# A new order for five engines ahead of the second feed-forward block, a second buffer for output gates, and one state copy on VectorE

## The chip, the cores and the metric

The kernel runs on one core of a Trainium2 chip, in one launch. The time is device time in microseconds, and the median of several runs is compared. A profile shows one further execution with its instructions: PE is TensorE, DVE VectorE, ACT ScalarE, POOL GpSimd, SP the engine whose queue issues the DMAs. PEld is TensorE's weight load.

## What is computed

The reference is an mLSTM attention with a running state, then two feed-forward layers over 3072 tokens (4 batches of 768) with 320 features:

```python
for t in range(S):
    m_new = np.maximum(f_gate[:, :, t] + m, i_gate[:, :, t])
    f_stab = np.exp(f_gate[:, :, t] + m - m_new)
    i_stab = np.exp(i_gate[:, :, t] - m_new)
    m = m_new
    C = f_stab[:, :, None, None] * C + i_stab[:, :, None, None] * np.einsum('bhd,bhe->bhde', vt, kt)
    n = f_stab[:, :, None] * n + i_stab[:, :, None] * kt
    h_tilde = np.einsum('bhde,bhe->bhd', C, qt)
    nq = np.einsum('bhd,bhd->bh', n, qt)[:, :, None]
    denom = np.maximum(np.abs(nq), 1.0)
    o = 1.0 / (1.0 + np.exp(-o_gate[:, :, t]))
    y[:, :, t] = o * h_tilde / denom
...
h = np.maximum(x @ w_in, 0.0)
x = (h * h @ w_out).astype(np.float32)
...
h = x @ w_in
g = h * (1.0 / (1.0 + np.exp(-h)))
return (g @ w_out).astype(np.float32)
```

Both feed-forward layers go from 320 features to 2048 and back.

## The kernel before

**Tiles.** The attention goes by chunks of 128 tokens: 24 tiles, numbered by the list `TILES`. Tiles 0 to 17 take the batches 0, 1 and 2 in turn, chunk by chunk; tiles 18 to 23 are batch 3. Tile 18 is therefore the only tile behind the first three that begins a batch. The first feed-forward layer runs over 8 blocks of 384 tokens (three tiles), each in 16 slices `in0` to `in15` of 128 columns, and an `out` step after each; the second layer runs over 3 blocks of 1024 tokens.

**The early part.** Everything up to the end of the first block's feed-forward (400 steps) is named, and each name has a date in the table `ORDER`. The steps are sorted by date, no earlier than what they need, and written out in that order for all five engines, so each engine runs its instructions in that order and waits where its next instruction has to wait. The program behind it keeps TensorE's order by hand too.

**The names.** A step's number after a colon is its tile, one without is a slice or a weight piece.
- Gates: `ga`, `gg` are VectorE's scans (line 219, 224) over the gates, `0` for the first 128 columns, `1` for the other 640; `ta`, `tb` are TensorE's transposes of them and `tc`, `td` VectorE's copies of these (line 246).
- Attention of a tile: `q`, `v`, `w`, `e` and `sg` are loads on SP; `b0`, `b1` masks and `s` scores on TensorE (lines 435 to 518); `x0`, `x1` exponentials on ACT (line 493); `d` VectorE's products of the two (line 526); `h` TensorE's weighted sums (lines 590 to 605); `ev` their division and gating (lines 616 to 624); `si` ACT's sigmoid of the output gates (line 415); `st`, `gr`, `gm` the state, where `gr` copies it out of PSUM (line 642 on); `xt`, `xa`, `xl` the transposition into the feed-forward's `x` and its split into a high and a low part. `stk` is a stacked operand of later tiles, which SP fetches by DMAs (`sj`).
- Weights of the first layer: 16 pieces; `L` loads piece k on SP, `P` (ACT), `D` (VectorE), `C` (ACT) and `M` (VectorE or POOL) split it into two parts (from line 287). Piece 0 feeds `in0` and `in1`, piece 1 `in2` and `in3`, piece 3 `in4` and `in5`, piece 5 `in6` and `in7`, piece 11 `in12` and `in13`.
- Slice j: `in` (TensorE, line 734) into PSUM, `r` relu, `gh` high part, `g` square (each on ACT, or `g` on VectorE or POOL), `gl` low part on VectorE (line 758), then `out` (lines 778 to 780).

**Padding.** `#x n` in the table puts n matmuls on a tile of zeros ahead of step x (`pad`, line 250), written into a PSUM buffer that the step overwrites; `warm` does the same as a step of its own (line 256).

Of the kernel before, what the change touches and what calls it, by code (L numbers as in the profile page):

```python
# [12 lines left out]
ACTF = mybir.ActivationFunctionType  # L13
# [41 lines left out]
    #h:3 3 #xt:4 3 tc0 3.01 b0:0 3.02 we0 3.18 tb0 3.3 td0 3.3 x0:0 3.53 x1:0 3.63 s:0 3.73 b0:1 3.9 b1:0 3.91
    b1:1 4 #warm1 4 s:1 4.2 L2 4.73 gD0 4.8 #in2 5 b0:2 5.1 s:2 5.18 b1:2 5.2 ga1 5.4 ee0 5.98 #xt:2 6 #ta1 6
    #in0 6 #in3 6 x0:1 6.1 d0:0 6.13 x1:1 6.2 #in4 7 warm1 8.02 x1:2 8.58 tb1 10.18 gb1 10.24 vk:0 10.78
    gg1 11.34 ee1 11.5 eD0 11.53 #warm7 12 gc1 12.02 gD1 12.19 eD1 12.19 ar1 13.07 x0:2 13.43 q:3 16.85 e:3 16.91
    we1 16.95 st:0 17.83 warm2 18.11 d0:1 19.97 w:3 20.45 P0 20.72 as1 20.84 wt1 20.84 ta1 20.84 d1:1 21.43
    d1:0 21.63 h0:0 21.85 h1:0 21.85 D0 22.18 vk:1 22.56 tc1 22.58 warm3 22.81 v:3 22.81 L3 23.49 h0:1 23.99  # L60
    vk:2 24.22 C0 26.17 h1:1 30.45 d0:2 31.5 td1 31.73 warm4 32.12 take 32.12 ev:0 32.4 xt:0 32.73 d1:2 32.73
    M0 32.87 sg:3 33.05 ev:1 33.8 q:4 33.92 h0:2 34.17 xa:0 34.3 P1 34.34 m1:3 34.54 m0:3 34.85 xl:0 34.92
    ev:2 35.22 h1:2 35.31 xt:1 35.48 D1 35.71 xt:2 35.72 P2 35.78 M3 36.13 mp 36.55 gr:0 37.3 xa:2 37.68
    xa:1 38.05 w:4 38.23 xl:1 38.41 warm5 38.43 L5 38.51 in0 38.51 gm:0 38.76 L4 38.83 st:1 38.88 x1:3 38.93
    e:4 39.13 xl:2 39.14 C1 39.19 M1 39.19 C2 39.28 warm6 39.31 x0:3 39.5 r0 39.55 gh0 39.55 in1 39.59 D2 39.66
    M2 39.73 g0 39.73 gl0 39.73 C3 39.75 s0:3 39.87 d0:3 39.87 gh1 39.87 P3 39.88 vv:3 39.88 r1 39.91 g1 40.14
    in3 40.17 in2 40.27 si:3 40.29 L6 40.89 out0 41.04 D3 41.13 g3 41.51 gl3 41.51 gr:1 41.97 r3 42.38 gh3 42.38
    vk:3 43.21 gl1 44.17 s1:3 44.78 m1:4 44.97 v:4 45.57 r2 46.1 P4 46.81 in4 49.09 st:2 49.18 L7 49.83 gh2 49.97
    gm:1 50.07 qt:3 50.24 P5 50.37 m0:4 50.44 D4 50.55 g2 50.82 d1:3 50.84 r4 50.89 gh4 50.89 q:5 50.94
    gr:2 51.16 vv:4 51.34 D5 51.43 C4 51.57 M4 51.73 g4 52 gm:2 52.19 gl4 52.23 gl2 52.57 in5 52.61 x0:4 52.91  # L70
    P6 53.16 C5 53.21 h:3 53.22 out1 53.27 D6 53.39 out2 53.73 ev:3 53.74 C6 54.24 M5 54.27 st:3 54.6 L8 54.81
    r5 54.83 m0:5 54.94 M6 55.46 w:5 55.46 P7 55.72 x1:4 56.86 gr:3 56.92 gm:3 56.92 in6 56.93 r6 57.24 gh6 57.24
    g6 57.24 L9 57.75 L10 59.56 P8 59.75 D7 59.78 m1:5 59.82 gl6 60.05 D8 60.25 xt:3 60.31 s0:4 60.36 C7 60.38
    d0:4 60.47 e:6 60.53 gh5 60.56 g5 61.18 gl5 61.18 x0:5 61.41 s1:4 61.58 d1:4 61.58 C8 61.68 M8 61.68
# [5 lines left out]
    gl9 70.23 r10 70.32 P12 70.33 P11 70.95 g10 71.2 v:6 71.38 gm:4 71.81 out8 71.98 q:7 72.53 gh10 72.55  # L80
    out7 72.61 xa:4 72.71 sj:6 72.74 d1:5 72.98 D11 73.07 C11 73.07 D12 73.19 C12 73.21 M12 73.21 M11 73.41
    st:4 73.61 gr:4 73.61 P13 73.7 in12 73.8 r12 73.83 D13 74.47 r11 74.86 gl10 75.12 g12 75.29 h:5 75.48
    gh12 75.52 P14 76.12 D14 76.12 C13 76.53 vk:5 76.55 g11 76.56 g13 76.78 in13 77.01 r13 77.02 M13 77.08
    gl11 77.18 gh11 77.29 gh13 77.39 m0:6 77.46 out9 77.54 gl13 77.55 out10 77.7 w:7 77.77 C14 77.79 in14 77.91
# [1317 lines left out]
```

## Time and profile before

| | us |
|---|---|
| runs | 803.69, 805.22, 806.42; median 805.22 |
| profiled execution | 803.72 |
| its span (first to last instruction) | 802.0 |
| TensorE busy | 794.4 |
| VectorE busy | 588.1 |
| ACT busy | 506.1 |
| POOL busy | 65.6 |
| granted clock of TensorE, mean | 1.00 |

The profile comes from the one execution of 803.72 us, so a sum made from its rows is made against that time. Times in rows count from the start of the span. An instruction's row on TensorE includes the part in which the next one already runs; how long a step holds the engine is therefore read from start to start.

### The profile page before, as it was taken

To read this page: it belongs to the slowest core of one execution; us is meant where nothing else is said; L and a number is where in the kernel's file an instruction comes from. 1 tells how busy PE (TensorE), PEld (TensorE's weight loads), DVE (VectorE), ACT (ScalarE), POOL (GpSimd) and SP (SyncE) were. 2 spreads that over 40 slices of the span, in tenths; PEclk is the share of its full clock that TensorE was granted. 3 is DMA by queue.
4 is the path that set the end of the run, shared out by engine and by line. 5 is a ranking of instruction groups with operands and counts; after the bars stand their busy time and mean duration, and the time that the engine had idled before them with its cause. 6 is when DMAs were issued, how large, how long until landed. Compare 5 with 4: busy or idle time off the path is not lost.

```text
span 802.0 us, 15413 instructions
## 1 busy us (share of the span) xinstructions
PE 794.4 (99%) x5671; PEld 748.0 (93%) x5671; DVE 588.1 (73%) x1117; ACT 506.1 (63%) x1018; POOL 65.6 (8%) x92
## 2 busy tenths in 40 slices
...
GB/s 259 241 249 277 174 160 194 223 212 254 237 229 257 230 226 252 193 240 236 200 107 128 239 204 219 200 181 162 45 152 129 154 152 121 80 142 128 64 34 34
DMA packets 110961, 144.63 MB, mean 180 GB/s; under 512 B 39567, under 2 KB 81431, under 8 KB 110887
## 3 DMA queue, kind: packets, MB, share of 16 engines
...
q8 instruction: 45, 0.74, 0.4%
...
## 4 chain that ended last, share of the span: by engine, by line
PE 94%; ACT 2%; DMA 2%; SPq 1%; issue 0%; DVE 0%; ACTq 0%
PE hin L734 21%; PE mC L875 15%; PE o L991 7%; PE o L990 7%; PE o L992 7%; PE o L778 7%; PE o L779 7%; PE o L780 7%; PE mA L875 3%; PE hA L605 2%; PE sc L518 2%; PE hA L590 2%; PE mO L875 1%; PE hA L600 1%; PE st L640 1%; PE xT L674 1%
## 5 line engine op out<-in xcount | busy, mean ns | idle before, releaser
L734 PE MATMUL hin<-x,wi 128*128 128x384 f32 x1024 | 203.2, 340 | 0.0
L734 PEld LDWEIGHTS hin<-x,wi 128*128 128x128 f32 x1024 | 177.6, 188 | 0.8 <-ACT r L742 0.2
L778 PE MATMUL o<-wo,gh 128*128 128x320 f32 x384 | 120.8, 315 | 0.0
L779 PE MATMUL o<-wo,gh 128*128 128x320 f32 x384 | 118.7, 309 | 0.0
L990 PE MATMUL o<-wo,gh 128*128 128x320 f32 x384 | 118.6, 309 | 0.0
L991 PE MATMUL o<-wo,gh 128*128 128x320 f32 x384 | 118.6, 309 | 0.0
L992 PE MATMUL o<-wo,gl 128*128 128x320 f32 x384 | 118.5, 309 | 0.0
L780 PE MATMUL o<-wo,gl 128*128 128x320 f32 x384 | 118.5, 308 | 0.0
L875 PE MATMUL mC<-xa,wp 128*128 128x512 f32 x396 | 113.6, 395 | 0.0
L742 ACT ACTIVATE r<-hin 128x384 f32<-128x384 f32 x128 | 61.9, 485 | 66.5 <-PE hin L734 66.2
L875 PEld LDWEIGHTS mC<-xa,wp 128*128 128x128 f32 x396 | 73.8, 189 | 15.7
L758 DVE TENSOR_TENSOR gl<-r,gh 128x384 fp32r<-128x384 f32 x128 | 70.5, 560 | 19.7 <-ACT r L753 19.3
L991 PEld LDWEIGHTS o<-wo,gh 128*128 128x128 f32 x384 | 72.2, 188 | 1.3
L990 PEld LDWEIGHTS o<-wo,gh 128*128 128x128 f32 x384 | 72.1, 188 | 1.3
L778 PEld LDWEIGHTS o<-wo,gh 128*128 128x128 f32 x384 | 72.1, 188 | 0.4 <-issue 0.2
L779 PEld LDWEIGHTS o<-wo,gh 128*128 128x128 f32 x384 | 72.2, 188 | 0.1
L780 PEld LDWEIGHTS o<-wo,gl 128*128 128x128 f32 x384 | 72.1, 188 | 0.0
L992 PEld LDWEIGHTS o<-wo,gl 128*128 128x128 f32 x384 | 72.1, 188 | 0.0
L746 ACT ACTIVATE gh<-r 128x384 fp32r<-128x384 f32 x128 | 67.2, 525 | 3.8
L753 ACT ACTIVATE r<-r 128x384 f32<-128x384 f32 x125 | 65.6, 525 | 3.9
L889 ACT ACTIVATE r<-c 128x512 f32<-128x512 f32 x24 | 15.2, 632 | 66.6 <-DVE c L911 66.6
L911 DVE TENSOR_TENSOR c<-u,mC 128x512 f32<-128x512 f32 x44 | 30.0, 687 | 33.7 <-PE mC L875 33.7
...
## 6 DMA issues: line engine op xcount, KB each, us to landing
...
```

The costliest lines, as they stand in the source:

```text
L734: pe.matmul(ps[:, 0:N], w[:, c, ws], x[:, sl, 0:N], start=(k == 0), stop=(k == 7))
L742: act.activation(out=r, in_=ps, func=ACTF.Relu)
L746: act.activation(out=gh, in_=r, func=ACTF.Square)
L753: act.activation(out=r, in_=r, func=ACTF.Square)
L758: on("gl", t0 // L).tensor_tensor(out=gl, in0=r, in1=f(gh), op=ALU.subtract)
L778: pe.matmul(o[k][:, 0:DM], gh[:, c], w[:, 0:320], start=first, stop=False)
L779: pe.matmul(o[k][:, 0:DM], gh[:, c], w[:, 320:640], start=False, stop=False)
L780: pe.matmul(o[k][:, 0:DM], gl[:, c], w[:, 0:320], start=False, stop=last)
L875: pe.matmul(o, w, x, start=start and k == 0, stop=k == 3, skip_group_check=True)
L990: pe.matmul(o[k][:, 0:DM], gh[:, t], w[:, 0:320], start=first and x == 0, stop=False)
L991: pe.matmul(o[k][:, 0:DM], gh[:, t], w[:, 320:640], start=False, stop=False)
L992: pe.matmul(o[k][:, 0:DM], gl[:, t], w[:, 0:320], start=False, stop=last and x == len(js) - 1)
```

## The change

It has four parts.

**1. The table `ORDER` is new**, all 400 dates. Two rows of it, for the look of it:

```diff
-    b1:1 4 #warm1 4 s:1 4.2 L2 4.73 gD0 4.8 #in2 5 b0:2 5.1 s:2 5.18 b1:2 5.2 ga1 5.4 ee0 5.98 #xt:2 6 #ta1 6
+    0.7 c0 0.92 warm7 0.94 #b0:0 1 #h:1 1 q:1 1.57 #warm9 2 c4 2.37 v:1 2.88 #xt:2 3.0 #in4 3.0 sg:0 3.35 c2 3.43
```

The padding matmuls go from 75 to 16:

| | before | after |
|---|---|---|
| ahead of the first gate transpose | `warm7` 12, `warm8` 1 | `warm7` 6, `warm9` 2 |
| up to `in0` | `b0:1` 2, `s:1` 1, `s:2` 3, `warm1` 4, `warm2` 2, `h:1` 3, `xt:2` 6, `st:1` 2, `in0` 6 | `b0:0` 1, `h:1` 1, `xt:2` 3 |
| behind it | `in1` 1, `in2` 5, `in3` 6, `in4` 7, `st:2` 3, `h:3` 3, `xt:3` 1, `s:4` 2, `s:5` 1, `xt:4` 3, `st:4` 1 | `in4` 3 |

What it does to the start of the program on SP, whose queue issues every load, is seen in its first rows. `kq` are keys and queries of a tile, `vk` and `x` values, `sg` output gates, `raw` a weight piece of 768 KB and `ro` one of 640 KB; the first `raw` before is piece 0, then 1. Before:

```order
L411 DMA sg<-in_og_dram 128x3x320
L387 DMA kq<-in_qkn_dram 40x2x512 x4
L402 DMA vk<-in_vk_dram 128x656 x2
L387 DMA kq<-in_qkn_dram 40x2x512 x2
L402 DMA x<-in_vk_dram 128x656
L268 DMA raw<-in_w_in_dram 128x1536 x2
L281 DMA ro_260<-in_w_out_dram 128x1280
L232 DMA g_d<-gg 32x128
L233 DMA e_d<-eg 32x128
```

After (the first `raw` is piece 1, the second piece 0):

```order
L386 DMA kq<-in_qkn_dram 40x2x512 x2
L401 DMA vk<-in_vk_dram 128x656
L410 DMA sg<-in_og_dram 128x3x320
L386 DMA kq<-in_qkn_dram 40x2x512 x4
L267 DMA raw<-in_w_in_dram 128x1536
L401 DMA vk<-in_vk_dram 128x656
L231 DMA g_d<-gg 32x128
L280 DMA ro_209<-in_w_out_dram 128x1280
L401 DMA x<-in_vk_dram 128x656
L267 DMA raw<-in_w_in_dram 128x1536
L231 DMA g_d<-gg 32x640
```

The load of piece 0 moved behind those of piece 1 and of the first `ro`.

On VectorE the long scans moved. Rows of the gates before (`COPY aw` is `tc0` and `td0`, `32x640` the other 640 columns):

```order
L228 TENSOR_TENSOR a_r<-a_r,gg 32x128
L229 TENSOR_TENSOR w_a<-a_r,gg 32x128
L246 COPY aw<-gT 128x32 x2
L219 SCALAR_TENSOR_TENSOR w_r<-fg,w_r,a_r 32x640
L526 TENSOR_TENSOR W<-sc,W 128x512
L221 TENSOR_TENSOR fg<-fg,w_r 32x640
L560 TENSOR_TENSOR vk<-vk,aw 128x320
L222 TENSOR_TENSOR fg<-fg,w_r 32x640
L224 SCALAR_TENSOR_TENSOR gg<-eg,fg 32x640
```

After:

```order
L218 SCALAR_TENSOR_TENSOR w_r<-fg,w_r,a_r 32x640
L227 TENSOR_TENSOR a_r<-a_r,gg 32x128
L220 TENSOR_TENSOR fg<-fg,w_r 32x640
L221 TENSOR_TENSOR fg<-fg,w_r 32x640
L226 TENSOR_TENSOR a_r<-a_r,w_r 32x640
L228 TENSOR_TENSOR w_a<-a_r,gg 32x128
L223 SCALAR_TENSOR_TENSOR gg<-eg,fg 32x640
L245 COPY aw<-gT 128x32
L227 TENSOR_TENSOR a_r<-a_r,gg 32x640
L525 TENSOR_TENSOR W<-sc,W 128x512
```

Both scans over 640 columns now stand ahead of the first `COPY aw`.

TensorE's row just ahead of the first feed-forward matmul (`hin`), before, from the transposition of tile 2 on; `wz` is the tile of zeros, and of the six pads ahead of `hin` the first is shown:

```order
L674 MATMUL xT<-ident,y 128x128 x2
L677 MATMUL xT<-ident,y 64x128 x2
L250 LDWEIGHTS wz
L250 MATMUL st<-wz 128x512
L250 LDWEIGHTS wz
L250 MATMUL st<-wz 128x512
L640 MATMUL st<-vk 120x126 x2
L640 MATMUL st<-vk 80x84
L250 LDWEIGHTS wz
L250 MATMUL hin<-wz 128x512
```

After, from the last of the three pads that stand ahead of that transposition:

```order
L249 LDWEIGHTS wz
L249 MATMUL xT<-wz 128x512
L676 MATMUL xT<-ident,y 128x128 x2
L679 MATMUL xT<-ident,y 64x128 x2
L639 MATMUL st<-x 120x126 x2
L639 MATMUL st<-x 80x84
L736 MATMUL hin<-x,wi_353 128x384 x16
L736 MATMUL hin<-x,wi_469 128x384 x8
```

The pads ahead of `hin` are gone, and the state matmuls of tile 2 (`st<-x`) stand there.

On ACT between the slices 2 and 4 of block 0, before (`sg<-sg` is the sigmoid `si:3`, the `wi` behind it `C3`, which leads to the weights of `in4`):

```order
L742 ACTIVATE r<-hin 128x384
L746 ACTIVATE gh<-r 128x384
L753 ACTIVATE r<-r 128x384
L415 ACT_TABLE_LOAD
L415 ACTIVATE sg<-sg 128x960
L320 ACTIVATE wi_616<-dt 128x768
L650 ACTIVATE cc_122<-st 120x252
L651 ACTIVATE cc_122<-st 80x84
L742 ACTIVATE r<-hin 128x384
L746 ACTIVATE gh<-r 128x384
L753 ACTIVATE r<-r 128x384
L742 ACTIVATE r<-hin 128x384
```

After (the first row is `r1`):

```order
L744 ACTIVATE r<-hin 128x384
L748 ACTIVATE gh<-r 128x384
L744 ACTIVATE r<-hin 128x384
L414 ACT_TABLE_LOAD
L414 ACTIVATE sg<-sg 128x960
L744 ACTIVATE r<-hin 128x384
L319 ACTIVATE wi_601<-dt 128x768
L748 ACTIVATE gh<-r 128x384
```

The relu of slice 2, which stood behind slice 3's work, stands ahead of the table load, and the relu of slice 3 ahead of `C3`.

**2. Five squares** (`g1`, `g7`, `g8`, `g10`, `g11`) go from ACT to VectorE, by entries of the table `PLAN`.

**3. Two buffers for the output gates.**

```diff
-        sg = T["sg", n] = at.tile([128, 3, DM], F32, tag="sg", name="sg", bufs=1)
+        sg = T["sg", n] = at.tile([128, 3, DM], F32, tag="sg", name="sg", bufs=2)
```

**4. The state copy of tile 18** (first chunk of its batch, tile number not under `N_NAT` = 6) goes from ACT to VectorE:

```diff
         if c == 0:
-            act.activation(out=cv[:, 0:6], in_=ps[0:120, 0:6], func=ACTF.Copy)
-            act.activation(out=cv[0:80, 6:8], in_=ps[0:80, 6:8], func=ACTF.Copy)
+            for m, hs in ((120, slice(0, 6)), (80, slice(6, 8))):
+                if i < N_NAT:
+                    act.activation(out=cv[0:m, hs], in_=ps[0:m, hs], func=ACTF.Copy)
+                else:
+                    dve.tensor_copy(out=cv[0:m, hs], in_=ps[0:m, hs])
```

VectorE's rows at that place after the change (`cc` is the state, `cm` its masked form, `gl` a slice's low part):

```order
L625 COPY y<-y 128x64
L760 TENSOR_TENSOR gl<-r,gh 128x384
L653 COPY cc_121<-st 120x252
L653 COPY cc_121<-st 80x84
L669 TENSOR_TENSOR cm<-cc_121,bmask 120x336
L760 TENSOR_TENSOR gl<-r,gh 128x384
```

The two copies stand between the `gl` and `cm`, where before `gl` was followed by `cm`.

## Rows read from the trace of the kernel before

**Rows 1.** Which share of the span each engine is busy (the page's first part).
```profile
PE 794.4 (99%) x5671; PEld 748.0 (93%) x5671; DVE 588.1 (73%) x1117; ACT 506.1 (63%) x1018; POOL 65.6 (8%) x92
```

**Rows 2.** The chain that ended last, share of the span (the page's fourth part).
```profile
PE 94%; ACT 2%; DMA 2%; SPq 1%; issue 0%; DVE 0%; ACTq 0%
```

**Rows 3.** TensorE's waits, whole run: line waited for, us in total, times, longest.
```profile
PE warm L256 <- DVE wz L1115: 1.1, 1, 1.1
PE xT L674 <- ACT cc L651: 0.9, 1, 0.9
PE sc L518 <- DMA stk<-tt: 0.5, 1, 0.5
```

**Rows 4.** Line 250's pads, 33.8 to 106: start:end length, PE busy (matmuls), weight loads, clock.
```profile
33.80:106.00 72.20, 9.43 (x35) 2.66 (x33) 1.00 0.67 223
```

**Rows 5.** Timeline of TensorE: start, us, line, operation, out<-in, count.
```profile
29.42 1.47 PE L250 MATMUL xT<-wz 128*128 128x512 bf16 x6
...
32.16 0.74 PE L640 MATMUL st<-vk 128*120 128x126 f32 x6
...
33.84 1.78 PE L734 MATMUL hin<-x,wi 128*128 128x384 f32 x8
...
44.82 1.68 PE L250 MATMUL hin<-wz 128*128 128x512 bf16 x7
46.15 1.06 PE L734 MATMUL hin<-x,wi 128*128 128x384 f32 x4
```

**Rows 6.** Timeline of VectorE, 8 to 34 us; idle time and its end in brackets.
```profile
8.55 1.53 DVE L219 TENSOR_TENSOR_SCAN w_r<-fg,w_r,a_r 32x640 f32<-32x640 f32 x1
...
12.56 1.90 DVE L224 TENSOR_TENSOR_SCAN gg<-eg,fg 32x640 f32<-32x640 f32 x1
...
20.83 0.56 DVE L293 TENSOR_SCALAR dt<-dt 128x768 int32<-128x768 int32 x1 [2.28 <-ACT dt L291]
...
22.54 0.68 DVE L526 TENSOR_TENSOR x<-sc,x 128x512 f32<-128x512 f32 x1
...
24.03 0.17 DVE L616 TENSOR_SCALAR den<-hA 128x8 f32<-128x8 f32 x1 [0.57 <-PE hA L600]
...
28.91 0.17 DVE L616 TENSOR_SCALAR den<-hA 128x8 f32<-128x8 f32 x1 [0.41 <-PE hA L600]
...
32.73 1.02 DVE L691 TENSOR_TENSOR x<-xT,x 128x384 fp32r<-128x384 f32 x2 [0.35 <-ACT x L687]
```

**Rows 7.** All engines by stretch: busy time (instructions), granted clock, DMA share, GB/s.
```profile
0.00:5.00 5.00, 3.94 (x12) 1.53 (x13) 1.42 (x6) 1.28 (x1) 4.01 (x20) 1.00 0.55 153
5.00:10.00 5.00, 3.98 (x33) 2.64 (x31) 2.59 (x7) 3.59 (x7) 1.29 (x7) 1.00 0.87 218
10.00:15.00 5.00, 5.00 (x48) 4.44 (x47) 4.96 (x7) 2.70 (x11) 0.98 (x2) 1.00 0.95 309
15.00:20.00 5.00, 4.70 (x40) 3.26 (x39) 3.52 (x6) 3.34 (x13) 0.76 (x1) 1.00 0.90 356
34.00:106.00 72.00, 72.00 (x496) 65.61 (x496) 62.66 (x110) 64.26 (x125) 25.82 (x23) 1.00 0.67 223
```

**Rows 8.** Timeline of ACT, 19 to 46 us.
```profile
19.89 0.91 ACT L291 ACTIVATE dt<-raw 128x768 f32<-128x768 f32 x1
...
40.25 1.28 ACT L415 ACT_TABLE_LOAD   x1
41.54 1.01 ACT L415 ACTIVATE sg<-sg 128x960 f32<-128x960 f32 x1
...
45.20 0.47 ACT L742 ACTIVATE r<-hin 128x384 f32<-128x384 f32 x1
```

**Rows 9.** Timeline of ACT around the state copy of tile 18.
```profile
326.11 0.36 ACT L650 ACTIVATE cc<-st 120x252 f32<-120x252 f32 x1
```

**Rows 10.** Timeline of VectorE around the state copy of tile 18.
```profile
324.62 0.56 DVE L758 TENSOR_TENSOR gl<-r,gh 128x384 fp32r<-128x384 f32 x1
326.62 0.51 DVE L667 TENSOR_TENSOR cm<-cc,bmask 120x336 f32<-120x336 f32 x1 [1.45 <-ACT cc L651]
```

More of the change, by code (lines that the diff above doesn't have):

```diff
@@ L55 @@
[L55 to L74, printed above, removed]
@@ L80 @@
[L80 to L84, printed above, removed]
@@ L90 @@
-    g17 93.75 gl16 94.36 m0:7 95.99 m1:7 97.39 in18 98.16 vv:7 99.49 gl17 99.53 g18 100.11 out15 100.66
-    r18 100.72 x0:7 101.14 gh18 101.4 gl18 102 x1:7 103 q:8 103.75
+    #warm0 0 #warm3 0 #warm4 0 #warm5 0 #warm6 0 #s:0 0 #h:0 0 #st:0 0 #xt:0 0 #b1:0 0 #xt:1 0 #b1:1 0 #h:2 0 #b0:2
+    0 #b1:2 0 #s:3 0 #st:3 0 #h:4 0 #h:5 0 #st:5 0 #xt:5 0 #warm8 0 #s:1 0 #xt:3 0 #st:4 0 #s:5 0 #in1 0 #warm2 0
+    #st:1 0 #b0:1 0 #s:4 0 #s:2 0 #st:2 0 #h:3 0 #xt:4 0 #warm1 0 #in2 0 #ta1 0 #in0 0 #in3 0 gates 0.62 c3 0.63 wz
@@ new lines @@
+    24.96 take 24.962 L3 24.964 m0:3 24.966 x1:3 25.0 st:1 25.09 sg:3 25.43 xt:2 25.67 gr:1 26.17 warm5 26.19 D1
+    26.192 v:3 26.51 xa:1 26.55 st:2 26.92 e:4 27.03 xa:2 27.04 xl:1 27.65 C1 27.78 mp 27.782 xl:2 28.12 in0 28.122
+    L5 28.51 x0:3 28.512 M1 28.65 w:4 29.03 L6 29.51 gm:1 29.59 gr:2 29.68 D2 30.01 in1 30.09 r0 30.29 P3 30.66 gh0
+    31.39 in2 31.5 v:4 31.51 D3 31.53 C2 31.8 e:6 31.99 r1 32.43 M2 32.57 s0:3 32.91 gh1 32.95 g0 33.0 r2 33.37 gl0
+    33.59 g1 33.74 vv:3 33.82 q:5 33.822 qt:4 34.06 gm:2 34.53 in3 34.66 gl1 34.95 d0:3 35.42 si:3 35.44 s1:3 36.02
```

54 lines of the change are left out of this document (36 added, 18 removed).

## The prediction

> **What bounds the kernel now.** I read the page first. TensorE is busy for 99% of the span [rows 1], and the chain of work that ended last is TensorE for 94% of it [rows 2]. So only what makes TensorE's row of instructions shorter, or what makes it wait, moves the end. Next come TensorE's waits over the whole run: the longest is 1.1 us at the start, then 0.9 us for ACT's copy at line 651, 0.5 us for a DMA of `stk`, and nothing else over 0.4 us [rows 3]. That looks like a kernel without waits, but the early part is not: 75 matmuls on a tile of zeros (`pad` and `warm`) stand in its row, and they cover waits. By the table of pads 13 stand ahead of the first gate transpose and 29 from there to the first feed-forward matmul; 33 more, by their weight loads, stand between 33.8 and 106 us [rows 4], where `out15` ends. Six pads take 1.47 us and seven take 1.68 [rows 5], so one more pad holds TensorE for 0.21 us; I use 0.215. The question of this case is what the pads cover: where a pad goes and the wait behind it stays, nothing is gained.
>
> Then I asked what sets the first feed-forward matmul. It starts at 33.84 [rows 5], 0.1 us after VectorE's last write of its `x`, `xl:2`, which ends at 32.73 + 1.02 = 33.75 [rows 6]. From the decode of weight piece 0 at 20.83 on, VectorE waits little: 0.57, 0.41 and 0.35 us [rows 6]. It is the engine that sets the start, and the pads in TensorE's row there hide that.
>
> **Part 1, the start up to `in0`.** The new order moves the long gate scans of VectorE (1.53 and 1.90 us [rows 6]) ahead of the small copy `tc0` that the first exponentials wait for; it moves the load of weight piece 0 (L0) behind pieces 1 and 2; and it moves the product `d0:2` ahead of that piece's decode. For the first: the exponentials of tile 0 come some 3.5 us later, but the decode of piece 0 was waiting 2.28 us for ACT anyway [rows 6], and behind ACT's exponentials of tile 2 at that. For the load: the loads up to and with piece 0 are now about 4.7 MB (their sizes stand in the new row of SP), and the DMAs moved 153, 218, 309 and 356 GB/s in the first four stretches of 5 us [rows 7]. That is 3.4 MB by 15 us and the rest 3.7 us later, at 18.7. Since SP lets eight DMAs be under way and waits between, I take 20.2. ACT's first pass over the piece is 0.91 us [rows 8], so VectorE begins the decode at 21.1. From 20.83 to 33.75 it had 12.9 us, of which 1.3 us were the idle times named above and 0.68 us was `d0:2` [rows 6]; 12.9 - 1.3 - 0.7 = 10.9, so `xl:2` would end at 32.0 and `in0` start at 32.1. **Gain 1.7 us.** Bounds: if the idle times stay it is 0.4; if the piece lands at 18.7 it is 3.2; if it comes 4 us later than the latest time that the old profile allows (19.89 [rows 8], 1.4 MB more ahead of it at 356 GB/s), `in0` comes at 35.8 and 2.0 us are lost. I take 1.7, nearest to the row of VectorE's own work.
>
> **Part 2, from `in0` to `out15`.** Removed: 33 pads of 0.215 us, 7.1 us; moved ahead of it: the six state matmuls of tile 2, some 0.5 us (0.74 with their tail for those of tile 1 [rows 5]). So 7.6 us come free if nothing waits. I then laid the measured durations into the new order, engine by engine, and looked where TensorE would stand. Five places are left:
> - `in4` waits for weight piece `M3`. In ACT's new row the sequence after `in3` is: table load and sigmoid, `r3`, then `C3`, and only then VectorE's `M3`. The table load takes 1.28 us and the sigmoid 1.01 [rows 8]. At 1.4 to 1.5 us for eight `in` matmuls, `in2` ends 4.4 us after the start of `in0`; `r2` 0.5, table 1.3, sigmoid 1.0, `r3` 0.5, `C3` 0.8 and `M3` 1.2 us follow, to 9.7 or 9.8 us. TensorE has done `s0:3` (1.1), `in3` (1.45) and `out0` (1.3) at 8.2. That is 1.6 us, with the three pads that stay there (0.65 us) inside it.
> - `in6` for `M5`, 0.4 us; `in12` for `M11`, 1.05 us; `in14` for its weight piece, 0.25 us.
> - `h:4` for VectorE's `d1:4`, 0.65 to 1.9 us, since `D8`, `gl5`, `M8` and `gl6` stand ahead of it.
>
> Together 3.95 to 5.2 us; I take 4.6. **Gain 7.6 - 4.6 = 3.0 us.** Bounds: zero waits would give 7.6, waits as long as all the pads 0.5 or less. The new waits are sums of rows in an order that has not run, so the error of each may be half of it. The second squares g1, g7, g8, g10 and g11 change from ACT to VectorE, about 5 x 0.55 = 2.8 us. ACT had 64.3 and VectorE 62.7 us of work in the 72 us of this stretch [rows 7]; in 69 us VectorE would have 65.5, 95%. It is why I take no more than 3.0 here.
>
> [...]
>
> **Part 3, two single waits.** TensorE waited 0.9 us once for ACT's copy at line 651 [rows 3]. The row is at 326.11 on ACT, behind exponentials and a weight scale that it has to finish first [rows 9], while VectorE stood idle for 1.45 us and waited for the same copy [rows 10]. Now VectorE makes the two copies itself, right behind `gl`, which ended at 325.2. VectorE's price for the copies is not in the old trace; ACT takes 0.36 us for the larger, and VectorE 0.56 for `gl`, which is larger still [rows 9, 10]. Two by at most 0.4 us end at 326.0, where ACT's ended at 326.6, so of TensorE's wait some 0.2 us or nothing is left: **gain 0.8 us**, bounds 0 and 0.9. The wait of `sc` for the DMA of `stk`, 0.5 us [rows 3], goes if the whole row of SP comes earlier with the rest: **gain 0.5 us**, bounds 0 and 0.5. The second buffer for the output gates lets their load start without waiting for the last reader; the sigmoid that it feeds starts after 40 us on ACT in both orders, so I cost it at nothing. It costs nothing if ACT is late anyway; that cover is there as long as ACT's table load stands behind `r2`.
>
> **The sum.** 1.7 + 3.0 + 0.8 + 0.5 = 6.0 us. Behind `out15` TensorE's row is the same and without waits but the ones named, so what is gained by then passes through to the end. The profiled execution is 803.7 (802.0 of span and 1.7 outside it); 803.7 - 6.0 = 797.7. The median of the runs shown is 805.2, 1.5 above the profiled one, so on that scale 799.2. About 0.3% (2.4 us) is what a measurement of this kernel can tell from no change, and the forecast is 0.75% below 805.2.
>
> **The rivals.**
> (a) All pads were waste and the new order brings no waits. For it: the row shows no place where TensorE stood behind a pad. Against it: the seven pads ahead of `in4` end at 46.15 [rows 5], and `r2`, which empties the PSUM buffer that `in4` writes, runs to 45.20 + 0.47 = 45.67 on ACT [rows 8], so most of these pads covered a wait. Time: 1.7 + 7.6 + 1.3 = 10.6 us, or 794.6.
> (b) No gain in the feed-forward and none at the start: new waits take the place of the pads. For it: VectorE at 95% as worked out above, POOL's 25.8 us in the same stretch [rows 7], a table load ahead of `C3`, and L0's later load. Against it: the start is paced by VectorE's own work, and that grows by nothing there. Only part 3 is left, 1.3 us: 803.9, within the 0.3%.
> (c) The other side: the clock of TensorE. The row now has only 8 warming matmuls ahead of the first real one where 13 were, and 5 pads from there to `in0`, where 29 stood. [...] In the new order I count it busy for about two thirds of 5 to 14 us, with no idle longer than about 1.5 us. [...] It decides if the granted clock is below 1 somewhere between 5 and 9 us; if it is, slower; if it is 1.00 there, this is out. [...]
> (d) The change does not do what it says at tile 18: the copies on VectorE come too late because `gl` before them waits. Then 0.8 us are missing, 800.0, inside the forecast's range.
>
> **How the numbers follow.** Forecast, 799.2 (with d): 0.60. (a) 0.08; (b) 0.20; (c) 0.12. Faster by over 0.3% is the forecast and (a): 0.68; same is (b): 0.20; slower is (c): 0.12. The range leaves out (c) and half of (a): from 795.0 to 804.5, which takes in (b) and the bounds of parts 1 and 2 (no wait at all to waits like the pads).
>
> **What would show it.** The first `hin` matmul at 32.1 +- 1.2; `out15` ending at about 101 where 105.97 stood; a wait of TensorE for the low half of a weight piece ahead of `in4`, of about 1 us; TensorE's waits in the first 110 us of 5 to 9 us in place of 4 us; VectorE's copy at about 325.5 and no wait of `xT` there; granted clock 1.00 from 5 to 35 us. Wrong would be: a granted clock below 1 in the start, `in0` after 33.8, or waits of TensorE between `in0` and `out15` over 7 us.

## The result, and the profile after

The changed kernel takes 816.57 us (814.61 to 818.28); the kernel before, in the same comparison, 804.46 us. The ratio is 1.0147, 95% interval 1.0115 to 1.0178: 12.1 us slower, where 799.2 was forecast. The profiled execution took 814.61 us, with a span of 812.6.

From the page of the changed kernel: busy time of the engines, the granted clock in 40 slices (tenths of full speed), and the chain that ended last.

```profile
PE 795.9 (98%) x5612; PEld 752.8 (93%) x5612; DVE 597.9 (74%) x1124; ACT 503.1 (62%) x1011; POOL 65.8 (8%) x92
...
PEclk9699999999999999999999999999999999999999
...
PE 89%; DVE 4%; DMA 3%; SPq 1%; issue 1%; ACT 1%; DVEq 0%
```

TensorE has 59 pads fewer and is busy for 1.5 us more than in [rows 1], and its share of the chain fell from 94% [rows 2] to 89%. One of the 40 clock slices reads 6, and the others hide what the finer stretches show. By stretch (columns as in [rows 7], the granted clock third from the end):

```profile
12.00:15.50 3.50, 3.50 (x23) 2.96 (x20) 0.69 (x1) 3.32 (x12) 0.00 (x0) 0.51 0.99 347
15.50:25.50 10.00, 9.46 (x93) 8.56 (x93) 6.40 (x11) 7.55 (x22) 1.64 (x3) 1.00 0.50 185
25.50:39.50 14.00, 14.00 (x67) 11.22 (x67) 8.33 (x21) 4.22 (x11) 3.28 (x4) 0.51 0.93 275
39.50:53.00 13.50, 10.23 (x69) 8.98 (x69) 13.10 (x19) 11.04 (x23) 6.78 (x6) 1.00 0.69 209
53.00:56.50 3.50, 3.50 (x13) 3.50 (x13) 3.43 (x7) 2.90 (x5) 0.00 (x0) 0.51 0.00 0
100.00:104.50 4.50, 3.77 (x15) 3.71 (x15) 4.33 (x11) 3.44 (x7) 0.45 (x1) 0.62 0.03 7
```

In four stretches the granted clock is at half, 0.50 in windows of 1 us inside them: 12.1 to 15.5, 25.7 to 39.4, 53.1 to 56.5 and 100.9 to 104.3 us. In the longest TensorE is counted busy throughout (14.00 of 14.00), and its row of three pads, from 36.25, takes 1.49 us, as long as the 1.47 of six in [rows 5]. The eight products of one mask step take 1.05 us ahead of the first fall and 1.92 in it:

```profile
7.33 1.05 PE L438 MATMUL wp<-gg,ident 128*128 128x128 f32 x8
13.65 1.92 PE L438 MATMUL wp<-gg,ident 128*128 128x128 f32 x8
```

One minus the granted clock, summed over the time up to 130 us, is 11.9 us. In the kernel before it was 0.

TensorE's waits, to be read beside [rows 3]:

```profile
PE hin L736 <- DVE wi L322: 5.0, 3, 3.3
PE sc L511 <- DMA kq<-in_qkn_dram: 2.8, 2, 2.3
PE o L782 <- DVE gl L760: 1.7, 1, 1.7
PE warm L255 <- DVE wz L1117: 1.1, 1, 1.1
PE hin L736 <- DVE wi L323: 0.7, 1, 0.7
```

Between `in0` and `out15` it waits 7.8 us, and 7.6 of them are for VectorE.

And its timeline at the start, which answers to [rows 5] (line numbers differ by one or two from those of before):

```profile
10.68 0.46 PE L511 MATMUL sc<-kq 40*128 40x128 f32 x2 [2.29 <-DMA kq<-in_qkn_dram]
11.67 1.65 PE L511 MATMUL sc<-kq 40*128 40x128 f32 x14 [0.54 <-DMA kq<-in_qkn_dram]
...
22.02 0.84 PE L639 MATMUL st<-vk 128*120 128x126 f32 x6 [0.54 <-ACT x L492]
...
39.66 0.74 PE L736 MATMUL hin<-x,wi 128*128 128x384 f32 x2
```

Between 8.39 and 11.67 TensorE waited 2.29 us and then 0.54 us for the keys of tile 0, and the first slow stretch follows at 12.1. From there to the second, at 25.7, its only wait is the 0.54 us at 22.02. The first `hin` matmul comes at 39.66, 5.8 us later than the 33.84 of before, and `out15` ends at 117.4, 11.4 us later than 105.97. From there to the end of the span it is 695.2 us, 0.8 less than before. So all of the loss lies ahead of 118 us, half of it ahead of `in0`.

In front of `in4` TensorE waited 3.3 us for VectorE's weight piece. One row of POOL, then VectorE's, there:

```profile
43.91 1.99 POOL L334 TENSOR_TENSOR wo<-dt,wo 128x640 fp32r<-128x640 f32 x1 [11.60 <-ACT wo L332]
```

```profile
44.42 1.90 DVE L753 TENSOR_TENSOR r<-r 128x384 f32<-128x384 f32 x1
...
46.83 0.99 DVE L753 TENSOR_TENSOR r<-r 128x384 f32<-128x384 f32 x1
47.74 0.98 DVE L571 TENSOR_TENSOR q<-q,eq 120x384 f32<-120x384 f32 x1
48.64 1.05 DVE L669 TENSOR_TENSOR cm<-cc,bmask 120x336 f32<-120x336 f32 x1
49.62 1.07 DVE L760 TENSOR_TENSOR gl<-r,gh 128x384 fp32r<-128x384 f32 x1
...
51.81 0.67 DVE L322 TENSOR_TENSOR wi<-dt,wi 128x512 fp32r<-128x512 f32 x1
```

A square of 128x384 takes 1.90 us beside POOL's 1.99 us, and 0.99 beside another; the median of VectorE's eight squares is 0.55. POOL's instruction ended at 45.90, the square at 46.32. `M3`, the row at 51.81, had these rows ahead of it, though its input from ACT was there at 48.56. Instructions like the last four of the five long rows shown take 0.51 to 0.56 us elsewhere in this run, with POOL idle beside them (from 41.26, 52.97, 83.61 and 84.08). At these lengths the five would take 2.7 us; they take 6.0, and the 3.3 us between are as long as TensorE's wait. Of the square's 1.90 us, 1.48 lie beside POOL's instruction and 0.42 behind its end, and 0.42 is most of the 0.55 that a square takes. What holds VectorE up beside POOL is not shown.

### The profile page after: what moved, and what is told of

Same layout as the page of the kernel before. It is cut to its first block, busy times and chain, and to the rows that moved or that the text cites. A ratio compares the mean times of both kernels' runs of the same rounds, so it can differ in the third digit from the quotient of the medians.

```text
span 812.6 us, 15296 instructions
## 1 busy us (share of the span) xinstructions
PE 795.9 (98%) x5612; PEld 752.8 (93%) x5612; DVE 597.9 (74%) x1124; ACT 503.1 (62%) x1011; POOL 65.8 (8%) x92
## 4 chain that ended last, share of the span: by engine, by line
PE 89%; DVE 4%; DMA 3%; SPq 1%; issue 1%; ACT 1%; DVEq 0%
PE hin L736 19%; PE mC L877 15%; PE o L992 7%; PE o L994 7%; PE o L993 7%; PE o L780 6%; PE o L782 6%; PE o L781 6%; PE mA L877 3%; PE hA L604 2%; PE sc L517 2%; PE mO L877 1%; PE hA L589 1%; PE hA L599 1%; PE st L639 1%
## 5 line engine op out<-in xcount | busy, mean ns | idle before, releaser
L736 PE MATMUL hin<-x,wi 128*128 128x384 f32 x1024 | 205.4, 342 | 6.0 <-DVE wi L322 5.0
L760 DVE TENSOR_TENSOR gl<-r,gh 128x384 fp32r<-128x384 f32 x128 | 72.9, 578 | 16.3 <-ACT r L755 15.9
L755 ACT ACTIVATE r<-r 128x384 f32<-128x384 f32 x120 | 63.1, 526 | 3.7
```

Of the source, the lines that this page charges most:

```text
L736: pe.matmul(ps[:, 0:N], w[:, c, ws], x[:, sl, 0:N], start=(k == 0), stop=(k == 7))
L755: act.activation(out=r, in_=r, func=ACTF.Square)
L760: on("gl", t0 // L).tensor_tensor(out=gl, in0=r, in1=f(gh), op=ALU.subtract)
```

## Experiments

Theory 1: the lower clock is the loss. Theory 2: later loads and VectorE's longer row are, and the clock fell only because TensorE had nothing to do. "Clock lost" is the sum of one minus the granted clock up to 130 us in the profiled execution; the first `hin` and the end of `out15` are from the same one. Each ratio, with its interval, is to executions of the kernel before that were measured along with that kernel; the median of before in the table is that of the first comparison.

| kernel | median us | ratio to before, 95% | clock lost | first `hin` | `out15` ends |
|---|---|---|---|---|---|
| before | 804.46 | | 0.0 | 33.84 | 105.97 |
| changed | 816.57 | 1.0147 [1.0115, 1.0178] | 11.9 | 39.66 | 117.41 |
| e1: changed, 22 pads at the start | 813.25 | 1.0108 [1.0087, 1.0128] | 8.5 | 38.19 | 115.80 |
| e2: changed, keys of tile 0 first | 820.05 | 1.0167 [1.0133, 1.0202] | 15.4 | 43.30 | 122.85 |
| e3: before, its first 13 pads alone | 806.68 | 1.0022 [1.0003, 1.0041] | 10.2 | 36.79 | 108.23 |
| e4: before, copy on VectorE | 804.33 | 0.9998 [0.9986, 1.0010] | 0.0 | 33.58 | 105.70 |
| e5: changed, 75 pads more | 809.20 | 1.0055 [1.0036, 1.0073] | 0.0 | 36.78 | 112.15 |
| e6: e5, squares on ACT | 810.79 | 1.0081 [1.0055, 1.0108] | 0.0 | 36.79 | 111.48 |
| e7: changed, gates as before | 817.58 | 1.0157 [1.0126, 1.0188] | 11.9 | 41.72 | 117.37 |
| e8: before, without the 33 later pads | 803.01 | 0.9978 [0.9959, 0.9997] | 0.0 | 33.53 | 104.61 |
| e9: e8, `r2` and `gl2` earlier | 803.66 | 0.9993 [0.9975, 1.0010] | 0.0 | 33.51 | 104.25 |
| e10: e5, `M3` earlier | 809.23 | 1.0054 [1.0039, 1.0068] | 1.7 | 37.91 | 112.82 |
| e11: e8 without nine more pads | 807.77 | 1.0033 [1.0022, 1.0044] | 6.8 | 39.16 | 109.60 |
| e12: before, two gate buffers | 804.48 | 1.0001 [0.9989, 1.0013] | 0.0 | 33.97 | 106.06 |
| e13: changed, 22 pads more, the old nine in their place | 809.46 | 1.0071 [1.0042, 1.0101] | 1.7 | 33.25 | 112.51 |
| e14: e13, 21 pads more | 812.13 | 1.0081 [1.0057, 1.0105] | 6.8 | 41.37 | 117.02 |
| e15: e13, squares on ACT | 810.13 | 1.0080 [1.0054, 1.0105] | 1.7 | 33.28 | 107.40 |
| e16: before, five squares on VectorE | 810.70 | 1.0067 [1.0040, 1.0094] | 5.1 | 33.67 | 113.24 |

### Does the clock make the loss, and does one wait make the clock fall? (e1, e2, e7)

```diff
e1
-    #s:0 0 #st:0 0 #h:0 0 #h:2 0
+    #s:0 14 #st:0 3 #h:0 2 #h:2 3
e2
-    q:0 3.83
+    q:0 1.5
e7
-    q:0 3.83 as0 5.78 wt0 8.31 ta0 6.91 tc0 9.25 we0 9.382 ga1 4.98
+    q:0 1.5 as0 4.79 wt0 4.8 ta0 4.9 tc0 4.91 we0 4.92 ga1 5.5
```

> The changed kernel with 22 more padding matmuls ahead of in0 and nothing else: s:0 gets 14 (over its wait of 2.3 + 0.5 us for the keys of tile 0), st:0 3 (over its wait of 0.5 us), h:0 2 and h:2 3. Theory 1 (the lower clock is what was lost at the start): granted clock 1.00 up to in0, the first hin matmul at 32.5 to 34 in place of 39.66, and the time about 6 us under the changed kernel's, 810. Theory 2 (the order of loads and VectorE's longer row are what was lost, and the clock fell only because TensorE had nothing to do): hin still at 38 or later and the time within 2 us of the changed kernel's 816.6.

> The changed kernel with one date changed: the keys of tile 0 (q:0) are loaded ahead of those of tile 1, as in the kernel before. No pad is added. Theory 1: s:0 starts at about 8.4 in place of 10.7; if the clock falls because of that one wait, it stays at 1.00 through 16 us and in0 comes 3 us earlier or more; if the second fall (25.7 us) has a cause of its own, the granted clock is 0.5 again from about 25 us and hin comes at 36 to 38. Theory 2 (the order of loads): the same start of s:0 and hin earlier by the 2.8 us of the wait, at any clock.

> The changed kernel with the start of two rows put back: the keys of tile 0 are loaded first, and VectorE finishes the first 128 gate columns, with tc0, ahead of the scan of the other 640. No pads added. Theory 1a (the first fall of the clock comes from TensorE standing idle behind the long scans and the late keys): no wait over 1 us up to 20 us and clock 1.00 there; in0 2 to 6 us earlier than 39.66. If the second fall at 25 us has a cause of its own, the clock is at half there again and in0 comes at 36 to 38.

e1 covers the waits and the clock stays at 1.00 up to 27.4 us, and then it falls as in the changed kernel, until 37.6 us; 3.3 us come back, not 6. The longest wait in the 15 us ahead of that fall is 0.56 us. In e2 the keys are there, `s:0` starts at 8.3, and TensorE stands longer than ever, for another operand:

```profile
PE gT L244 <- ACT w_a L230: 5.5, 1, 5.5
```

In e7 that operand is early too, and the wait moves once more, to the first exponentials. TensorE, then ACT:

```profile
15.45 0.58 PE L434 MATMUL wp<-nmask,idb 128*128 128x512 bf16 x1 [5.36 <-ACT W L492]
```

```profile
11.95 1.00 ACT L414 ACTIVATE sg<-sg 128x960 f32<-128x960 f32 x1 [4.49 <-DMA sg<-in_og_dram]
12.96 1.28 ACT L492 ACT_TABLE_LOAD   x1
14.26 1.14 ACT L492 ACTIVATE W<-wp,aw 128x128 f32<-128x128 f32 x4
```

ACT waited 4.49 us for the output gates `sg:0`, whose sigmoid stands ahead of the exponentials in its new row, with a table load of 1.28 us behind it. In the changed kernel the sigmoid, the next table load and the first exponentials stand at 9.89, 10.91 and 12.42, in the kernel before at 5.48, 6.50 and 8.01. So three things are late there one behind the other: the gates land at 9.9, the keys at 11.5, and the copy `tc0` behind the long scans comes at 10.7. Taking one away shows the next. The guess that the keys alone make the first fall is wrong, and so is theory 1 as e1 put it: the second fall needs no fall ahead of it.

### What holds the clock? (e3, e11)

e3 takes all 62 pads behind the first transpose from the kernel before, e8 the 33 behind the first `in`, and e11 these and nine more:

```diff
e11, against e8
-    #warm1 4 #warm2 2 #h:1 3
+    #warm1 0 #warm2 0 #h:1 0
```

> The kernel before with the 62 pads behind the first gate transpose taken out, its order left as it was (the 13 warming matmuls stay). The prediction's rival (a), pads were waste: clock 1.00, and up to 13 us less, 791 to 800. Theory 1 (pads hold the clock): the granted clock falls below 1 at one or more places up to 106 us and the time is over 806. Theory 2 (pads only fill waits): clock may fall, but the end moves by less than 2 us.

> e8 without nine more pads: the four of warm1 and two of warm2 around 19 to 21 us and the three ahead of h0:1. Pads before and behind them stay. Question: does the second fall of the clock (25.7 us in the changed kernel, 21.9 in the kernel before without pads) need a long wait of TensorE ahead of it? Theory 1b (no: the row of transposes and weighted sums at 19 to 26 us, of 32 and 42 columns, brings it even where TensorE hardly waits): the clock falls between 21 and 27 us, no wait over 1.3 us stands ahead of it, and in0 comes 2 to 5 us later than e8's 32.4. Rival (the fall needs the long waits of the changed order): clock 1.00 and in0 within 1 us of e8's.

Without pads the old order has no end at 791 to 800 either: the clock is at half from 21.8 to 42.3 us, the first `hin` comes 3 us later, and the time is 806.68. e11 shows how little it takes. TensorE in e11, where the clock falls at 22.9:

```profile
20.02 0.84 PE L638 MATMUL st<-vk 128*120 128x126 f32 x6 [1.23 <-ACT x L491]
20.79 0.49 PE L243 MATMUL gT<-ident,a_r 32*128 32x32 f32 x5
...
21.82 2.51 PE L598 MATMUL hA<-vk,W 128*128 128x42 f32 x15
```

and in e8, where it does not:

```profile
18.49 1.03 PE L254 MATMUL warm<-wz 128*128 128x512 bf16 x4
19.89 0.84 PE L638 MATMUL st<-vk 128*120 128x126 f32 x6 [0.37 <-ACT x L491]
20.56 0.59 PE L254 MATMUL warm<-wz 128*128 128x512 bf16 x2
...
23.63 0.82 PE L248 MATMUL hA<-wz 128*128 128x512 bf16 x3
```

The stretch from 22 to 36 us in e11, then in e8:

```profile
22.00:36.00 14.00, 14.00 (x66) 11.28 (x67) 8.11 (x23) 3.19 (x6) 4.23 (x5) 0.53 0.42 138
```

```profile
22.00:36.00 14.00, 14.00 (x102) 11.02 (x103) 11.31 (x28) 7.66 (x19) 3.94 (x5) 1.00 0.70 213
```

The nine pads of 128x512 hold TensorE for some 2 us. Without them the clock falls amid transposes with 32 columns and sums with 42, after a wait of 1.23 us and none over 0.13 us behind it; the first `hin` comes 5.6 us later and the ratio goes from 0.9978 to 1.0033, 4.4 us. Theory 1b has the fall and the wait right and the delay of `in0` too small (2 to 5 us), and its rival falls. The second fall of the changed kernel comes at the same place of the row; that kernel has left out eight of the nine. The clock fell behind waits of 1.23 us (e11) and 0.54 us (the changed kernel), while TensorE was counted busy. Whether it was the narrow matmuls that did it is not shown; e11 takes the pads away from wait and matmuls alike.

### How much is the clock? (e5, e10, e13, e14)

```diff
e5
-    #s:0 0 #st:0 0 #h:0 0 #h:1 1 #xt:0 0 #h:2 0 #xt:1 0 #st:1 0 #xt:2 3.0 #in0 0 #in4 3.0
+    #s:0 14 #st:0 6 #h:0 4 #h:1 5 #xt:0 2 #h:2 4 #xt:1 2 #st:1 2 #xt:2 4 #in0 2 #in4 23 #in14 14
e10, against e5
-    #in4 23 C3 36.7 M3 37.57 qt:4 34.06 gm:2 34.53
+    #in4 8 C3 35.43 M3 35.432 qt:4 39.0 gm:2 39.1
e13
-    #s:0 0 #st:0 0 #h:1 1
+    #s:0 14 #st:0 6 #h:1 3
e14, against e13
-    #in4 3.0
+    #in4 20 #in14 4
```

> The changed kernel with its order as it is and 66 more padding matmuls: over the waits seen in its trace (s:0 14, st:0 6, in4 23, in14 14) and in small numbers (0 to 5, on h, xt, st and in0) between 22 and 40 us. Theory 1 (the clock, which is at half in four stretches up to 105 us and takes 11.9 us by the sum of one minus the granted clock): clock 1.00 throughout, the end of out15 at 105 to 108 in place of 117.4, time 804 to 807. Theory 2 (the waits themselves are the loss): clock 1.00, but out15 after 112 and time over 810.

> e5 (the changed kernel with pads that hold its clock) with four dates changed: ACT's C3 stands ahead of the table load of the sigmoid, VectorE's M3 ahead of gl3, qt:4 and gm:2 and of one product, and in4 has 8 pads in place of 23. Theory (in4 waits for M3 because it stands behind VectorE's row, which POOL's instructions stretch): in4's weights come 3 us earlier after in0 than in e5, and out15 ends 2 to 3 us earlier, 806 to 807.5. Rival (VectorE is the bound whatever stands first): in4 earlier, but the later waits grow by as much and out15 stays within 1 us of e5's 112.15.

> The changed kernel with 22 more pads and no others: 14 on s:0, and the old nine pads of 19 to 26 us (6 ahead of st:0, where warm1 and warm2 stood, and 2 more, in all 3, ahead of h0:1). If these nine hold the clock in the changed order too: clock 1.00 up to 50 us and in0 at 33.5 to 35.5; the time 2 to 4 us under e1's 813.3. If they are too few in this order: the clock falls between 26 and 32 us and in0 comes at 36 to 38, as in e1.

> e13 with 20 pads ahead of in4 and 4 ahead of in14 as well, over the two waits behind which the clock fell at 53 and 101 us. Theory (e5's 4.7 us over the kernel before are the order's own waits in the feed-forward stretch, 3.5 us, and less than 2 us of surplus pads at the start): clock 1.00, in0 at 34 to 35.5, from there to the end of out15 75 us as in e5, time 807 to 808.5. Rival (the 4.7 us are surplus pads): 804 to 805.5.

e5 has 75 pads more than the changed kernel, 91 in all (its expectation counts 66). It runs at 1.00 throughout, in all of its nine executions, and takes 809.2: of the 12.1 us, 7.4 come back with the clock and 4.7 do not. It missed theory 1's 804 to 807, by surplus pads at the start or by the order, and its `out15`, at 112.15, is where theory 2 had it. e13 tells these apart: with the nine old pads and the cover on `s:0` the clock holds up to 95.5 us, and

```profile
33.25 0.44 PE L736 MATMUL hin<-x,wi 128*128 128x384 f32 x1
```

the first `hin` comes at 33.25. The new order of the start, at full clock, is worth 0.6 us, or 0.3 to 0.7 beside e4 and e12, which have the old start (33.58 and 33.97). Yet `out15` ends at 112.5, as in e5 with its first `hin` at 36.8 and in e10 with 37.9. So 3.5 us at the start are given back behind it. Two things in the trace come to as much. The clock is at half from 95.5 to 98.9 us, 1.7 us, as it never is in e5. And the load of weight piece 3 hardly comes earlier with the start: SP issues it at 29.68 us, at 30.68 in the changed kernel, and ACT waits for it with its row:

```profile
38.35 0.91 ACT L290 ACTIVATE dt<-raw 128x768 f32<-128x768 f32 x1 [2.17 <-DMA raw<-in_w_in_dram]
```

Behind that TensorE waits 1.2 us at `in3` and 0.6 at `out0`. That these two are the whole reason is not shown. Nor does the clock hold in every execution of e13: four of ten took 812.8 to 820.1 us at a mean clock of 0.983 to 0.987, six 807.8 to 810.1 at 0.996 to 0.998, so that the 809.46 of the table lies between two groups. The six have 53 pads fewer than e5, and their median, 808.4, is 0.8 us under e5's. With the 1.7 us of lower clock in the one that was traced, surplus pads would be some 2.5 of e5's 4.7 us; that is an estimate. In e10 `M3` did come earlier and the wait ahead of `in4` went; a wait of 2.2 us for another weight piece at 55 us took its place, and its rival holds.

e14 failed as a measure: in its profiled execution the keys landed later, so that the 14 pads did not reach over the wait:

```profile
11.96 0.46 PE L511 MATMUL sc<-kq 40*128 40x128 f32 x2 [0.52 <-DMA kq<-in_qkn_dram]
13.14 1.16 PE L511 MATMUL sc<-kq 40*128 40x128 f32 x14 [0.72 <-DMA kq<-in_qkn_dram]
```

The clock then fell at 26.6 us. Of its nine executions, four took 806.9 to 810.4 us at a mean clock of 0.997 or more, and five 812.1 to 814.4 us at 0.989 to 0.992. That is one kernel with its clock held and lost, as in e13. The four lie nearer to its theory (807 to 808.5) than to its rival (804 to 805.5).

### What sets the end of the first block? (e6, e15, e16, e8, e9)

e6 and e15 put the five squares back on ACT; e16 gives them to VectorE in the old order.

```diff
e6, e15 (the list of squares on VectorE)
-    ... gm7 y7 vk8 g1 g7 g8 g10 g11
+    ... gm7 y7 vk8
```

> e5 with the five squares g1, g7, g8, g10 and g11 back on ACT. The prediction's rival (b), VectorE as the bound of the feed-forward stretch: in4's weights, written by VectorE, are ready 0.5 to 1.5 us earlier after in0 than in e5, and the time is 1 to 3 us under e5's. If VectorE's load is not what in4 waits for, or ACT becomes late instead: within 1 us of e5.

> e13 with the five squares g1, g7, g8, g10 and g11 back on ACT (e6 asked this, but there 23 pads ahead of in4 held TensorE longer than its weights did). In e5, e6, e10 and e13 out15 ends at 111.5 to 112.8, whether the first hin comes at 33 or at 38. If VectorE's row sets that end: out15 at 109 to 111 and the time 1.5 to 3 us under e13's 809.5. If it is set by loads or by ACT: out15 at 112 to 113 and the time within 1 us of e13's.

> The kernel before with part 2 of the change alone: the five squares on VectorE, its order and its 75 pads as they were. If VectorE has room in the old order (62.7 us of work in 72): within 1 us of the kernel before. If its row is already what TensorE's pads wait for: 1 to 3 us slower, with a wait for gl or a weight piece between 40 and 100 us.

e6 told nothing: its 23 pads ahead of `in4` ran longer than the weights needed, and four of its ten executions took 814.2 to 815.5 us at a mean clock of 0.996. e15 has the answer in its profiled execution: `out15` ends at 107.4 in place of 112.5, and that execution took 803.83. The rows of all engines from the first `hin` to the end of `out15`, of the changed kernel, of e13 and of e15:

```profile
39.66:117.40 77.74, 69.92 (x461) 65.44 (x460) 72.42 (x119) 60.96 (x117) 29.22 (x24) 0.96 0.62 202
```

```profile
33.25:112.50 79.25, 69.66 (x461) 63.90 (x460) 73.34 (x120) 61.27 (x117) 29.03 (x24) 0.98 0.68 219
```

```profile
33.20:107.00 73.80, 69.04 (x460) 63.42 (x458) 69.57 (x115) 62.60 (x122) 29.63 (x24) 0.98 0.72 235
```

VectorE has 62.7 us of work there in the kernel before [rows 7], 72.4 in the changed one, 73.3 in e13 and 69.6 in e15. It is busy for 93% of the stretch in the changed kernel and in e13, and with five instructions of it gone `out15` ends 5.1 us earlier in the executions traced. TensorE's waits for VectorE in the stretch are 7.8 us in e13 and 3.6 in e15: in these VectorE's row sets that end. The squares alone are not the 5.1 us. Piece 3 lands earlier in e15 (ACT takes it at 37.26, 1.1 us earlier than in e13), and one weight row of VectorE, for `in14`, meets POOL in e13 (a row of 1.83 us from 92.75) and not in e15:

```profile
93.12 2.02 DVE L322 TENSOR_TENSOR wi<-dt,wi 128x512 fp32r<-128x512 f32 x1
```

```profile
89.86 0.68 DVE L322 TENSOR_TENSOR wi<-dt,wi 128x512 fp32r<-128x512 f32 x1
```

e15's other four executions took 807.9 to 813.5 us at a clock of 0.987 to 0.995, so its median shows no gain; that it would keep 803.8 with the clock held is argued from the trace, not measured.

e16, part 2 of the change alone, costs 0.7% (0.4 to 0.9%). TensorE's steps stand where they stood before up to 79 us; then `in12` waits for piece 11, and the clock falls. VectorE's rows (the square `g10`, then the decode of piece 11, which stood at 78.48 before), ACT's `C11`, TensorE's wait, and the stretch behind it:

```profile
79.40 0.56 DVE L751 TENSOR_TENSOR r<-r 128x384 f32<-128x384 f32 x1 [1.89 <-ACT gh L746]
...
81.35 0.55 DVE L293 TENSOR_SCALAR dt<-dt 128x768 int32<-128x768 int32 x1
```

```profile
82.92 0.84 ACT L320 ACTIVATE wi<-dt 128x768 fp32r<-128x768 f32 x1 [3.18 <-DVE dt L294]
```

```profile
PE hin L734 <- ACT wi L320: 1.7, 1, 1.7
```

```profile
85.00:95.00 10.00, 10.00 (x42) 10.00 (x42) 7.67 (x14) 5.16 (x9) 3.33 (x3) 0.53 0.39 122
```

The square is not dear by its 0.56 us. On VectorE it waits 1.89 us for ACT's `gh10`, and the decode of piece 11 is queued behind it; 0.6 of the 1.89 are ACT's own wait for a weight load in this execution. That is 2.9 us later for a piece, 1.7 us of waiting for TensorE, and 5.1 us of lower clock behind the wait: 7.3 us at `out15`. It is more than the 1 to 3 us expected, by the clock. So VectorE can be late in two ways, by the sum of its work and by a step that waits in its row; e15 does not separate these in the changed order, where its row has 5.3 us of idle time in 77.7.

```diff
e8, against before
-    #in1 1 #in2 5 #in3 6 #in4 7 #st:2 3 #h:3 3 #xt:3 1 #s:4 2 #s:5 1 #xt:4 3 #st:4 1
+    #in1 0 #in2 0 #in3 0 #in4 0 #st:2 0 #h:3 0 #xt:3 0 #s:4 0 #s:5 0 #xt:4 0 #st:4 0
e9, against e8
-    r2 46.1 gl2 52.57
+    r2 40.285 gl2 50.825
```

> The kernel before, without the 33 pads behind the first in; the 42 ahead of it stay. The prediction's part 2 taken alone, with the old order: 7.1 us of pads gone. If waits that the pads covered take about half (as in the run without any pad, where the stretch from in0 on was 0.7 us shorter with 5 us of it at half clock): clock 1.00, out15 2 to 4 us earlier, 801 to 803. If the clock falls in the waits: 804 to 808. If pads were waste: 797.5.

> e8 (the kernel before without its 33 later pads) with two steps moved: ACT's r2 stands ahead of the table load of the sigmoid si:3, as in the changed order, and VectorE's gl2 right behind its square. In e8 TensorE waits 1.7 us for r2 ahead of in4 and 1.2 us for gl2 ahead of the end of out2. Theory (ACT and VectorE pace the feed-forward stretch, so that a step moved forward only hands the wait to the next): the wait for r2 goes, C3 and M3 come 0.5 us later, and at most 1 us of the 2.9 is gained: 802 to 803. Rival (the two waits are single misplacements): 2 to 3 us less than e8, 800 to 801.

e8 asks the same of the old order: what are the 33 later pads worth? TensorE's waits in it:

```profile
PE hin L732 <- ACT r L740: 1.7, 1, 1.7
PE o L778 <- DVE gl L756: 1.2, 1, 1.2
...
PE hin L732 <- ACT wi L318: 0.8, 1, 0.8
```

Of 7.1 us of pads, 1.0 us came off the stretch from `in0` to `out15`; 6.1 came back as waits. It can be followed by steps: up to `in4` 19 pads, some 4 us, are gone, but `in4` starts only 2.05 us earlier behind `in0`, since a wait of 1.7 us stands there. The time, 803.0 against 804.4, is 0.2% under the kernel before (0.03 to 0.4%), the lowest of all, by an interval that only just leaves out no change. e9 removes the two longest of these waits, and others take their place (1.3 us for a weight piece at 42 us, 0.7 at 49 us): 803.7, no gain on e8.

### Parts 3 and 4 of the change alone (e12, e4)

```diff
e12
-        sg = ... name="sg", bufs=1)
+        sg = ... name="sg", bufs=2)
e4
-            act.activation(out=cv[:, 0:6], in_=ps[0:120, 0:6], func=ACTF.Copy)
...
+                    dve.tensor_copy(out=cv[0:m, hs], in_=ps[0:m, hs])
```

> The kernel before with part 3 of the change alone, two buffers for the output gates. The prediction put it at nothing: SP's load of the gates of block 1 no longer waits at 25.5 to 30 us, and the time is within 1 us of the kernel before. Rival: the loads behind it on SP come earlier and in0 with them, over 1 us less.

> The kernel before with part 4 of the change alone: the state copy of tile 18 on VectorE. The prediction's part 3: TensorE's wait of 0.88 us for line 651 is gone or under 0.2 us, 0.8 us less. Rival: VectorE does the copies late and the wait stays at 0.5 us or more, no gain. In the time 0.8 us is under what a run can tell; the wait in the trace decides.

Two buffers cost and bring nothing, as forecast. In e4 VectorE makes both copies at 324.84, where ACT began at 326.11 [rows 9]; and TensorE waits at the same place for something else:

```profile
324.84 0.56 DVE L654 COPY cc<-st 120x252 f32<-120x252 f32 x2
```

```profile
326.30 0.86 PE L518 MATMUL sc<-stk 120*128 120x128 f32 x6 [1.29 <-DMA stk<-tt]
```

The wait for `xT` is gone, and the scores just ahead of it wait 1.29 us for the DMA of `stk`, which SP issued 0.4 us later in this run. No gain alone. In the changed kernel neither wait is there, and the time behind `out15` is 0.8 us shorter than before. One pair of executions is rough: over the traces this time is 694.1 to 696.2 us, 695.0 in the mean, in the ten kernels with the changed order, and 695.6 to 697.8, 696.4 in the mean, in the eight with the old one.

## Why the prediction was wrong

- **The clock.** This step failed. It stood as rival (c) with a chance of 0.12, because I worked out no idle over 1.5 us in the start and let only long waits count. Idle came to 2.3 us, since the keys of tile 0 landed 6 us after their issue. And the place that I named as decisive, 5 to 9 us, was wrong: the clock was 1.00 there, fell at 12.1, and fell for the longest time at 25.7 us behind no long wait. e11 shows that a pad's worth in this kernel is not its own time: nine of them, 2 us, are worth 4.4. I read pads as cover for waits alone, so I priced their removal at 0.22 us each, and rows 4 and 5 could not contradict it, because the clock was 1.00 in every row of before. Holding the clock gives back 7.4 of the 12.1 us (e5).
- **Part 1, the start.** 1.7 us were forecast; 5.8 were lost. At full clock the order gives 0.6 (e13). VectorE's row was right: 10.9 us were worked out from the decode of piece 0 to the last `xl`, and at full clock e13 takes 11.0 from the decode (22.26) to the first `hin` (33.25). In the changed kernel, with the clock at half, it is 16.9. SP's eight loads under way show in the trace of before: its fifteenth load, `ro`, waited 0.6 us for the seventh, a `kq`, and was issued at 10.41. The landing of piece 0 was near (20.2 taken, 20.5 measured), but ACT reached the piece at 21.8, because its exponentials came late, and the decode began at 22.8 where 21.1 was worked out; I had laid out VectorE and left ACT's row as it was.
- **Part 2, the stretch.** The waits were put at 4.6 us. In e13 TensorE's steps from `in0` to `out15` take 77.8 us from start to start; in the kernel before they take 70.6, or 63.0 without the 7.6 us that the forecast set free. Of the 14.7 us between, 0.65 are pads and 1.7 lower clock; 12.4 are left, and 9.6 of them are idle time in the trace. Where the other 2.8 went was not traced. The term that failed is VectorE's load: 65.5 us were worked out, 72 to 73 measured. The five squares were put at 2.8; VectorE's squares take 4.5 us more than before in the changed kernel and 4.1 in e13. The rest are four or five further instructions in the stretch (119 and 120, squares and all, for 110) and the rows that POOL stretched. Rival (b) named VectorE at 95% and a table load ahead of `C3`. That VectorE is what TensorE waits for was right (7.6 of 7.8 us), and it was capped at no gain without a reason. The wait of `in4`, 1.6 forecast, was 3.3 behind three pads: the sum put `M3` straight behind `C3`, and it stood in VectorE's row for 3.25 us more (48.56 to 51.81).
- **Rival (a)** is out by e3 and e8: pads were not waste, and without 33 of them 1.0 of 7.1 us is gained.
- **The two single waits, and the gates.** Near: 0.8 us less behind `out15` in the pair of executions, 1.4 in the mean of all traces, where 1.3 were forecast, and two buffers for the gates at nothing. e4 adds that the copy alone gains nothing.
- **The range** reached to 804.5. The clock and VectorE both went the same way, and I had treated them as separate cases of which only one can come. The three signs of being wrong all came: a clock below 1 in the start, `in0` at 39.66, and 7.8 us of waits between `in0` and `out15`. In the first 110 us TensorE is idle for 12.8 us, where 5 to 9 were given; before it is 2.5, not 4.

What stays open: e15's one execution at 803.8 is the nearest that the new order came to the old one; whether it can be held there was not tried. What in TensorE's row decides the clock at 22 us is not settled beyond the nine pads. Of the 4.7 us that do not come back with the clock, VectorE's row, the load of piece 3 and surplus pads can each have a part; the parts are not measured one by one.
